# The first pair of blocks of the second part by eight out-products, with the weight sums formed beside them

## The chip, the cores and the metric

The kernel runs on one core of a Trainium2 chip. The metric is the device time of one execution in microseconds (us); lower is better. Engines are named as in the profile: PE is TensorE, DVE is VectorE, ACT is ScalarE, POOL is GpSimd, SP is SyncE, which issues most transfers.

## The reference

A Fourier layer is followed by two feed-forward layers over 6016 tokens of width 256. The change touches the last one only:

```python
def _moe2_ref(x, w_gate, w_val, w_out):
    g = x @ w_gate                          # 256 -> 1536
    silu = g * (1.0 / (1.0 + np.exp(-g)))
    val = x @ w_val                         # 256 -> 1536
    return (silu * val @ w_out).astype(np.float32)   # 1536 -> 256
```

## The kernel before

Every product is made in float32 precision by three matmuls over a split `x = hi + lo`, `w = hi + lo` (`mm3`: lo·hi, hi·hi, hi·lo; only the third reads the low half of x). The last layer, here called the second part, is computed with tokens in six pairs of blocks (`pairs`; a block has 512 tokens, in the last pair 448) and the 1536 inner rows in twelve slices of 128. One pair with one slice is a unit; `quads2` lists the 72 units, pair by pair, and unit q belongs to pair q // 12. Units 0 to 11 are the first pair, units 12 to 23 the second.

A unit makes gate and value of two blocks by seven products of Strassen's kind (`product(P, 1)` and so on), 21 matmuls, into three PSUM banks called P, T (`Tb`) and Q. In between ACT copies P to Q (the copy that starts Q, line 1297), T to `c7`, P to `cu`; DVE adds `h0 = T + cu` (line 1351) and `h1 = P + c7` (line 1368), ACT takes SiLU of both, and DVE multiplies them with Q and with P (`times2`). The last product, 3, of a unit and its `times2` are made in the next unit (`upper`). The two results of a unit are the gated values of its two blocks, and the second matrix w_out turns them into the output.

For w_out the kernel before uses, in all pairs but the last, seven products over two units at a time (an even one and the odd one behind it): three are made in the pair itself (`live`, 3 matmuls in an odd unit, 6 in an even one), and four are made in the pair behind it (`later`, 6 matmuls in each of its units, from tiles `mid` that `part2` splits). The sums of gated values come from DVE (`add_up`) and from accumulating transfers of POOL (`add_apart`, line 1251). Seven products need sums of the weights of w_out: `out_sums` (four DVE operations on 128x128 and one of ACT) and `out_parts` (two casts, two subtractions, two transfers) form them once, in the first pair. The last pair uses `plain` units: eight products, 12 matmuls in each unit (`share`), straight from the gated values: `parted` splits each into `hi` (ACT) and `lo` (DVE).

All order is written out by hand: each engine runs its instructions in the order of the code. `todo.send` sends one step of the split of the next pair's x per unit: first its load (`raw`, line 840), in the units behind it a cast `xo` or `xy` on ACT (line 806) in some and one subtraction on DVE in each. `fetch` loads a slice's weights into one of four slots.

Of the kernel before, what the change touches and what calls it, by code (L numbers as in the profile page):

```python
# [82 lines left out]
def fourier_moe_kernel(ctx: ExitStack, tc: tile.TileContext, x, lin, bias, w1, w2, fwd1, inv2, fwd2,  # L83
# [1149 lines left out]
    fourth = {}  # L1233

    def out_parts(k):
        g = G.pop(k)
        t = cv.tile([128, 4, 2, 128], F32R, tag="full", name="parts", bufs=2)
        f = fourth[k] = cv.tile([128, 2, 128], F32R, tag="s4", name="s4", bufs=1)
# [37 lines left out]

    def quad(q, before):
# [3 lines left out]
        old, i = p - 1, f  # L1281
        a = (p, k - 1) if k else (p - 1, NK - 1)
        if q == 0:
            fetch(F0 + 2)
            fetch(F0 + 3)
        P, T, Q = bank_p(F0 + q), one_bank(spot[0] + 3, [128, BLK], "Tb"), bank_q([128, BLK], "Q")
        product = multiply(B[len(pairs) + p], F0 + q, n)
        product(P, 1, start=True)
        if old >= 0:
            later(old, i, 0)  # L1290
        else:
            if q == 0:
                mark(Q)
                end = end_of()
                drain(2)
# [4 lines left out]
        if old >= 0:  # L1300
            later(old, i, 1)
        if odd:
            x1 = halve(p, k, "T1")
            (add_up if p else add_apart)(p, k, "T1", "T3")
            if a[0] >= 0:
                add_up(*a, "T2", "T1")
                add_apart(*a, "T4", "T2")
        elif a[0] >= 0:
            x2, x3 = halve(*a, "T4"), halve(*a, "T2")
            add_up(*a, "T3", "T2")  # L1310
        if old >= 0 and i % 3 == 2:
            phase(old, i // 3)
        if old >= 0:
            product(T, 7, start=True)
        c7 = ring2["c"]()[:, :n]
        nc.scalar.copy(c7, T[:, :n])
        if q == 0:
            end()
        product(Q, 2)
        if q == 0:  # L1320
            drain(2)
        product(P, 6)
        if p == 0:
            if odd and k < NK - 1:
                out_parts(k)
            if f in (0, 2, 4, 6, 8, 9):
                out_sums((f + 1) // 2)
            if f == NF - 1:
                ask(0, 0)
                ask(0, 1)  # L1330
        else:
            ask(old + (i + 2) // NF, (i + 2) % NF)
        if old + (i + 1) // NF >= 0:
# [3 lines left out]
        if q == 0:  # L1337
            drain(2)
        if odd:
            live(p, 1, k, slot[F0 + q - 1][:, 14:16], x1)  # L1340
            free.append(slot.pop(F0 + q - 1))
            fetch(F0 + q + 3)
            if f == NF - 1:
                then = begin(p)
        elif a[0] >= 0:
# [4 lines left out]
        h0 = take("h")  # L1350
        nc.vector.tensor_tensor(out=h0[:, :n], in0=T[:, :n], in1=cu, op=ALU.add)  # L1351
        nc.scalar.activation(h0[:, :n], h0[:, :n], AF.Silu)  # L1352
        if q == 0:
            drain(len(pending))
            lay_out_rest()
        if not odd and a[0] >= 0:
            live(a[0], 3, a[1], slot[F0 + q - 1][:, 16:18] if a[0] else fourth[a[1]], x3)
            free.append(slot.pop(F0 + q - 1))
            fetch(F0 + q + 3)
            if not k:  # L1360
                third(a[0])
            if f == NF - 2 and not p:
                out_parts(NK - 1)
        if q == 2:
            mark(one_bank(spot[0], [128, BLK], "D"))
        product(P, 5)
        h1 = take("h")
        nc.vector.tensor_tensor(out=h1[:, :n], in0=P[:, :n], in1=c7, op=ALU.add)  # L1368
        if q == len(quads2) - NF:
            d = home.pop()  # L1370
            spots["own"] = [d[:, 0], d[:, 1]]
            state["own"] = take("own")
        times2(state["own"][:, :n] if p == len(pairs) - 1 else U(p, ("T1", "T4")[odd], k), h0[:, :n], Q[:, :n], -1 if odd else 1)
        todo.send()
        nc.scalar.activation(h1[:, :n], h1[:, :n], AF.Silu)
# [3 lines left out]

    def plain(q, before):  # L1380

        p, f = quads2[q] if q < len(quads2) else (None, None)
        pb, old, i = len(pairs) - 1, len(pairs) - 2, f
        n = halves[pb]
        _, _, _, Pb, hb, last, _ = before
        w = slot[F0 + q - 1]

        def share(t, e, x):
            if q == len(quads2) - NF + 1:
                where = acc_bank  # L1390
                if t and e:
                    def where(shape, name):
                        return bank_p(F0 + q)
                acc[t, e] = where([128, BLK], f"acc{t}{e}")
            mm3(acc[t, e][:, :n], w[:, 14 + 2 * e], w[:, 15 + 2 * e], *x, q == len(quads2) - NF + 1, p is None)

        def parted(x):
            hi, lo = (take(c)[:, :n] for c in ("hi", "lo"))
            nc.scalar.copy(hi, x[:, :n])
            low(lo, x[:, :n], hi)  # L1400
            return hi, lo

        early = f == 1
# [3 lines left out]
        last(Pb, 3)  # L1407
        s1 = take("own")
        times2(s1[:, :n], hb[:, :n], Pb[:, :n], 1)
        if p is not None and not early:  # L1410
            later(old, i, 0)
            later(old, i, 1)
        x0 = parted(state["own"])
        if p is None:
            x1 = parted(s1)
            for t, x in enumerate((x0, x1)):
                for e in range(2):
                    share(t, e, x)
                    a = acc.pop((t, e))
                    if t and e:  # L1420
                        for o, c, copy, send in ((take("short"), slice(0, n // 2), nc.vector.tensor_copy, nc.sync),
                                                 (take("h"), slice(n // 2, n), nc.scalar.copy, nc.scalar)):
                            copy(o[:, c], a[:, c])
                            at = pairs[pb][0] + n
                            send.dma_start(out[e * 128 : e * 128 + 128, at + c.start : at + c.stop], o[:, c])
                    else:
                        o = spots[("one", "short", "short", "three")[2 * t + e]].pop()
                        (nc.vector.tensor_copy if e else nc.scalar.copy)(o[:, :n], a[:, :n])
                        send_out(pb, e, t, o)
            return None  # L1430
        k, odd = divmod(f, 2)
        if f == 1:
            add_up(old, NK - 1, "T2", "T1")
            add_apart(old, NK - 1, "T4", "T2")
        P, T, Q = Pb, one_bank(spot[0] + 3, [128, BLK], "Tb"), bank_q([128, BLK], "Q")
        P = one_bank(spot[0] + 1 + (F0 + len(quads2) - NF) % 2, [128, BLK], "P")
        product = multiply(B[len(pairs) + p], F0 + q, n)
        product(P, 1, start=True)
        nc.scalar.copy(Q[:, :n], P[:, :n])
        x1 = parted(s1)  # L1440
        if i % 3 == 2:
# [4 lines left out]
        share(0, 0, x0)  # L1446
        product(Q, 2)
        product(P, 6)
        if i + 1 < NF:
            part2(old, i + 1)  # L1450
        if i + 2 < NF:
# [3 lines left out]
        share(0, 1, x0)  # L1455
        product(T, 4)
        h0 = take("h")
        nc.vector.tensor_tensor(out=h0[:, :n], in0=T[:, :n], in1=cu, op=ALU.add)
        nc.scalar.activation(h0[:, :n], h0[:, :n], AF.Silu)
        product(P, 5)  # L1460
        h1 = take("h")
        nc.vector.tensor_tensor(out=h1[:, :n], in0=P[:, :n], in1=c7, op=ALU.add)
        share(1, 0, x1)
        share(1, 1, x1)
        free.append(slot.pop(F0 + q - 1))
        fetch(F0 + q + 3)
        state["own"] = take("own")
        times2(state["own"][:, :n], h0[:, :n], Q[:, :n], 1)
        nc.scalar.activation(h1[:, :n], h1[:, :n], AF.Silu)
# [6 lines left out]
    for q in range(len(quads2)):  # L1476
# [3 lines left out]
        before = (plain if q > len(quads2) - NF else quad)(q, before)  # L1480
# [62 lines left out]
```

## Time and profile before

| what | value |
| --- | --- |
| median of three runs (lowest, highest) | 1128.63 us (1128.04, 1129.52) |
| the profiled execution | 1129.65 us, its span 1127.9 us |
| PE, DVE, ACT busy, share of the span | 98%, 87%, 72% |
| units 1 to 11 | 622.69 to 696.09 us |
| units 12 to 23 | 696.09 to 779.80 us |

A unit's edge is where PE starts its first product in the timeline. A busy PE is not PE at its peak, since the recorded matmuls overlap: each stands for 0.38 us, while they start every 0.22 us where nothing waits. So gaps are read from the starts of matmuls in the timeline and not from busy time.

### The profile page before, as it was taken

What the parts mean: (1) busy time and instruction counts of PE and PEld (TensorE: products, weight loads), DVE (VectorE), ACT (ScalarE), POOL (GpSimd) and SP (SyncE); (2) the same over time, 40 slices, a digit from 0 to 9 for tenths busy, and PEclk for the clock granted to TensorE, in tenths of its full rate; (3) what the DMA queues carried; (4) which work ended last, traced back from release to release, by engine and by line L of the source; (5) the groups of instructions that cost most, each with busy time, mean ns of one, the idle gap of its engine ahead of it and who ended that gap; (6) DMA issues with size and microseconds to landing.
All of it is one profiled execution on the core that took longest, in us unless ns stands there. A gap on an engine that the chain in (4) does not pass through costs nothing.

```text
span 1127.9 us, 20014 instructions
## 1 busy us (share of the span) xinstructions
PE 1104.3 (98%) x7380; PEld 969.3 (86%) x7380; DVE 982.1 (87%) x1723; ACT 810.8 (72%) x1499; POOL 82.1 (7%) x117
## 2 busy tenths in 40 slices
PE   8999999999999999999999898999999999999998
PEld 8989888888888888888899776888888888888997
DVE  6878888999999999999988788899999999998665
ACT  4767676788787787877777666777777777677655
POOL 3000015200000000000000122000000000000000
PEclk9999999999999999999999999999999999999999
DMA  7757335864483573653654898877877877787561
GB/s 295 291 181 230 121 111 183 279 229 152 143 274 116 181 260 112 224 186 137 217 207 142 239 283 261 264 238 232 266 245 227 268 242 236 236 247 247 196 210 66
DMA packets 83929, 238.90 MB, mean 212 GB/s; under 512 B 8372, under 2 KB 30548, under 8 KB 72376
## 3 DMA queue, kind: packets, MB, share of 16 engines
q1 hardware_dynamic: 75472, 217.77, 57.3%
q0 software_dynamic: 8064, 19.66, 7.1%
q8 instruction: 58, 0.95, 0.3%
q14 instruction: 39, 0.32, 0.1%
q10 hardware_dynamic: 296, 0.20, 0.1%
HBM read 182.55 MB, written 45.61 MB: 202 GB/s over the span
## 4 chain that ended last, share of the span: by engine, by line
PE 79%; DVE 7%; issue 5%; DMA 5%; ACT 3%; POOL 1%; SPq 0%; POOLq 0%; ACTq 0%; DVEq 0%
PE acc L133 8%; PE acc L134 8%; PE acc L135 8%; PE P L947 7%; PE P L949 6%; PE P L948 6%; PE Tb L949 3%; PE Tb L947 3%; PE Tb L948 3%; DMA raw<-Xd 2%; PE p L462 2%; PE D L1174 2%; PE D L1173 2%; PE D L1172 2%; PE p L368 2%
## 5 line engine op out<-in xcount | busy, mean ns | idle before, releaser
L618 ACT CAST gated<-r 128x512 fp32r<-128x512 f32 (+1 forms) x160 | 98.1, 613 | 64.8 <-DVE r L995 63.3
L138 DVE TENSOR_TENSOR gated<-r,gated 128x512 fp32r<-128x512 f32 (+1 forms) x160 | 107.9, 674 | 24.1 <-ACT gated L618 19.6
L133 PE MATMUL acc<-gated,w_o 128*128 128x512 f32 (+1 forms) x320 | 120.4, 376 | 0.0
L135 PE MATMUL acc<-gated,w_o 128*128 128x512 f32 (+1 forms) x320 | 119.6, 374 | 0.0
L134 PE MATMUL acc<-gated,w_o 128*128 128x512 f32 (+1 forms) x320 | 119.6, 374 | 0.0
L1352 ACT ACTIVATE hv<-hv 128x512 f32<-128x512 f32 (+1 forms) x61 | 38.4, 630 | 98.2 <-DVE hv L1351 98.2
L991 ACT ACTIVATE r<-hold,consts 128x512 f32<-128x512 f32 (+1 forms) x120 | 85.5, 713 | 14.3 <-DVE hold L999 12.2
L947 PE MATMUL P<-xo,slot 128*128 128x512 f32 (+1 forms) x240 | 91.2, 380 | 2.8 <-DVE hold L999 1.2
L948 PE MATMUL P<-xo,slot 128*128 128x512 f32 (+1 forms) x240 | 88.8, 370 | 0.0
L949 PE MATMUL P<-xo,slot 128*128 128x512 f32 (+1 forms) x240 | 88.8, 370 | 0.0
L1251 POOL DMA_DIRECT2D units<-units x36 | 30.8, 893 | 785.5 <-PE P L949 419.5
L995 DVE SCALAR_TENSOR_TENSOR r<-r,hold 128x512 f32<-128x512 f32 (+1 forms) x120 | 80.8, 673 | 2.5 <-ACT r L991 1.4
L133 PEld LDWEIGHTS acc<-gated,w_o 128*128 128x128 f32 x320 | 60.5, 189 | 7.0
L135 PEld LDWEIGHTS acc<-gated,w_o 128*128 128x128 f32 x320 | 60.5, 189 | 6.8
L134 PEld LDWEIGHTS acc<-gated,w_o 128*128 128x128 f32 x320 | 60.5, 189 | 6.7
L1152 ACT CAST parts<-units 128x1024 fp32r<-128x1024 f32 x60 | 63.1, 1052 | 0.0
L1248 DVE TENSOR_TENSOR units<-units 128x512 f32<-128x512 f32 x84 | 55.7, 687 | 6.3 <-DMA units<-units 5.4
L947 PEld LDWEIGHTS P<-xo,slot 128*128 128x128 f32 x240 | 45.3, 189 | 14.6 <-DVE hv L1368 3.9
L1267 ACT CAST live<-units 128x512 fp32r<-128x512 f32 x90 | 53.5, 615 | 0.5 <-DVE units L1255 0.2
L949 PEld LDWEIGHTS P<-xo,slot 128*128 128x128 f32 x240 | 45.4, 189 | 4.3
L948 PEld LDWEIGHTS P<-xo,slot 128*128 128x128 f32 x240 | 45.4, 189 | 4.2
L1368 DVE TENSOR_TENSOR hv<-P,cc 128x512 f32<-128x512 f32 (+1 forms) x61 | 41.7, 683 | 4.5 <-PE P L949 4.5
(263 smaller groups left out, 3385.6 us busy)
## 6 DMA issues: line engine op xcount, KB each, us to landing
slot<-Wd SPq DMA_DIRECT2D x48, 1024.0 KB
slot<-Sd SPq DMA_DIRECT2D x40, 896.0 KB
slot<-Wd SPq DMA_DIRECT2D x24, 1152.0 KB
st<-in_w SPq DMA_DIRECT2D x68, 256.0 KB
chunk<-Vd SPq DMA_DIRECT2D x60, 256.0 KB
Wd<-slot SPq DMA_DIRECT2D x12, 1024.0 KB
units<-units POOLq DMA_DIRECT2D x36, 256.0 KB, 7.8
m<-in_fwd SPq DMA_DIRECT2D x12, 512.0 KB
```

Source lines behind the costliest of these rows:

```text
L133: nc.tensor.matmul(o, wl, xh, start=start, stop=False)
L134: nc.tensor.matmul(o, wh, xh, start=False, stop=False)
L135: nc.tensor.matmul(o, wh, xl, start=False, stop=stop)
L138: nc.vector.tensor_tensor(out=o, in0=full, in1=hi.bitcast(F32), op=ALU.subtract)
L618: nc.scalar.copy(hi[:, :n], g[:, :n])
L947: nc.tensor.matmul(o, wl, hi, start=start, stop=False, skip_group_check=not start)
L948: nc.tensor.matmul(o, wh, lo, start=False, stop=False, skip_group_check=not start)
L949: nc.tensor.matmul(o, wh, hi, start=False, stop=True, skip_group_check=not start)
L991: nc.scalar.activation(r[:, :n], x[:, :n], AF.Relu, bias=three)
L995: nc.vector.scalar_tensor_tensor(out=r[:, :n], in0=r[:, :n], scalar=6.0, in1=x[:, :n], op0=ALU.min, op1=ALU.mult)
L1152: nc.scalar.copy(hi, t[:, :, :n])
L1248: nc.vector.tensor_tensor(out=o, in0=o, in1=U(p, x, k), op=ALU.add)
```

## The change

Pair 0 now runs in `plain` units too. Its gated values go to `share` at once, 12 matmuls a unit, and nothing of pair 0 is left for pair 1: no `live`, `add_up`, `add_apart`, `part2` and `later` of pair 0, and none of the chunks of weight sums that pair 1 loaded for it. `out_sums` and `out_parts` stay in pair 0, one of them at the end of each unit. Unit 12 is a `quad` that also makes the last shares of pair 0 (`first`) and sends its four outputs. In pair 1, odd units take another bank for Q, and the SiLU of `h1` is put behind the next unit's copy to Q (`silu`, `seed`). One of two single matmuls that only mark a bank is dropped.

```diff
@@ fetch
+                whole = p in (0, len(pairs) - 1)
...
-            if stream[q][0] == 2 and p == len(pairs) - 1:
+            if stream[q][0] == 2 and whole:
                 nc.sync.dma_start(to[:, 16 * 128 :], src[:, 18 * 128 :])
@@ helpers
+    def outward(p, t, e):
+        n = halves[p]
+        o, a = (spots["one"][-1], spots["short"][-1], spots["short"][-2], spots["three"][-1])[2 * t + e], acc.pop((t, e))
+        (nc.vector.tensor_copy if e else nc.scalar.copy)(o[:, :n], a[:, :n])
+        send_out(p, e, t, o)
+
+    def silu(q, x):
+        def act():
+            nc.scalar.activation(x, x, AF.Silu)
+
+        if NF <= q + 1 < 2 * NF:
+            state["silu"] = act
+        else:
+            act()
+
+    def seed(q, P, Q, n):
+        nc.scalar.copy(Q[:, :n], P[:, :n])
+        state.pop("silu", lambda: None)()
@@ quad
-        P, T, Q = bank_p(F0 + q), one_bank(spot[0] + 3, [128, BLK], "Tb"), bank_q([128, BLK], "Q")
+        P, T = bank_p(F0 + q), one_bank(spot[0] + 3, [128, BLK], "Tb")
+        if p == 1 and odd and f < NF - 1:
+            Q = one_bank(spot[0], [128, BLK], "Q")
+        else:
+            Q = bank_q([128, BLK], "Q")
...
-        if old >= 0:
+        if waits:
             later(old, i, 0)
...
-        nc.scalar.copy(Q[:, :n], P[:, :n])
-        if before:
+        seed(q, P, Q, n)
+        if first:
+            x0 = parted(state["own"], n)
+            x1 = parted(upper_plain(before), n)
+        else:
             upper(before)
...
+        if first:
+            share(q, 0, 0, x0)
+            outward(0, 0, 0)
         product(Q, 2)
...
         h1 = second_sum(P, c7, n)
+        if first:
+            outward(0, 1, 1)
+            home.append(spots["double"])
@@ plain
+        if before:
+            s1 = upper_plain(before)
...
+        if before:
+            x0 = parted(spots["own"][0], n)
...
+        seed(q, P, Q, n)
+        if before:
+            x1 = parted(s1, n)
...
         product(T, 7, start=True)
...
+            share(q, 0, 0, x0)
         product(Q, 2)
         product(P, 6)
...
+            share(q, 0, 1, x0)
         product(T, 4)
         h0 = first_sum(T, cu, n)
...
         product(P, 5)
         h1 = second_sum(P, c7, n)
+        if q:
+            share(q, 1, 0, x1)
+            share(q, 1, 1, x1)
+            gone(q - 1)
+        times2(take("own")[:, :n], h0, Q[:, :n], 1)
+        state["own"] = spots["own"][-1]
+        todo.send()
+        silu(q, h1)
+        if not p:
+            (out_parts if odd else out_sums)(k)
@@ main loop
-        before = (plain if q > len(quads2) - NF else quad)(q, before)
+        before = (plain if q < NF or q in LAST else quad)(q, before)
```

On DVE, from the `h0` of unit 2 on, stood before (`outs<-` are the weight sums, `xo<-` is the step for the next pair, `units<-hv,P` the `times2` of product 3, `live`, `lows` and `hv<-units` the low halves):

```order
L1351 TENSOR_TENSOR hv<-Tb,cc 128x512
L1368 TENSOR_TENSOR hv<-P,cc 128x512
L1255 TENSOR_TENSOR units<-hv,Q 128x512
L138 TENSOR_TENSOR xo<-raw_7220,xo 128x512
L1257 SCALAR_TENSOR_TENSOR units<-hv,P 128x512
L138 TENSOR_TENSOR hv<-units,live 128x512
L1248 TENSOR_TENSOR units<-units 128x512
```

The same place on DVE now:

```order
L1321 TENSOR_TENSOR hv<-Tb,cc 128x512
L1327 TENSOR_TENSOR hv<-P,cc 128x512
L1254 TENSOR_TENSOR units<-hv,Q 128x512
L138 TENSOR_TENSOR xo<-raw_7217,xo 128x512
L1224 SCALAR_TENSOR_TENSOR outs<-hv 128x128
L1224 SCALAR_TENSOR_TENSOR outs<-outs,hv 128x128
L1222 TENSOR_TENSOR outs<-hv 128x128
L1222 TENSOR_TENSOR outs<-hv,outs 128x128
L1254 TENSOR_TENSOR units<-hv,P 128x512
L138 TENSOR_TENSOR live<-units,live 128x512
L138 TENSOR_TENSOR lows<-units,live 128x512
```

The weight sums, which stood ahead of `h0`, stand between the two `times2` now, and the low half of the first block's gated values (`live`) behind them.

On PE, from the last product of unit 2 (`P<-xy`, the product 5) to the first share of unit 3 stand now (`acc_7270` and `acc_7274` are the shares of the second block, `P<-gs` the product 3 of unit 2, then the products 1 and 7 of unit 3):

```order
L950 MATMUL P<-xy,slot 128x512
...
L135 MATMUL acc_7270<-hv,slot 128x512
...
L135 MATMUL acc_7274<-hv,slot 128x512
...
L950 MATMUL P<-gs,slot 128x512
...
L950 MATMUL P<-xy,slot 128x512
...
L950 MATMUL Tb<-xy,slot 128x512
L133 MATMUL acc_7246<-live,slot 128x512
L134 MATMUL acc_7246<-live,slot 128x512
L135 MATMUL acc_7246<-live,slot 128x512
```

Of each product's three matmuls only the last is shown. Fifteen matmuls, and two more of `acc_7246` itself, stand between the end of product 5 and the first reader of that low half; before, the units of pair 0 had no share there.

## Rows read from the trace of the kernel before

**Rows 1.** The page, part 1: busy time, share of the span, instructions.

```profile
PE 1104.3 (98%) x7380; PEld 969.3 (86%) x7380; DVE 982.1 (87%) x1723; ACT 810.8 (72%) x1499; POOL 82.1 (7%) x117
```

**Rows 2.** Windows: each engine's busy time, unit 1 to 11, then 12 to 23.

```profile
622.69:696.09 73.40, 64.46 (x282) 51.65 (x280) 61.37 (x114) 48.63 (x97) 17.63 (x23) 1.00 0.88 271
696.09:779.80 83.71, 82.54 (x379) 70.96 (x378) 76.57 (x111) 59.43 (x101) 4.87 (x6) 1.00 0.78 239
```

**Rows 3.** Timeline of PE: first and last of 185 matmuls without a wait.

```profile
741.17 0.38 PE L1173 MATMUL D<-parts,chunk 128*128 128x512 f32 x1
...
780.88 0.38 PE L1174 MATMUL D<-parts,chunk 128*128 128x512 f32 x1
```

**Rows 4.** Waits from 614 to 785 us: total, times, longest.

```profile
DVE units L1248 <- DMA units<-units: 5.4, 3, 2.4
...
PE Q L947 <- ACT Q L1297: 4.2, 10, 0.6
```

**Rows 5.** Timeline, all engines, around the end of unit 5.

```profile
654.08 0.38 PE L949 MATMUL Tb<-gs,slot 128*128 128x512 f32 x1
...
654.57 0.69 DVE L1351 TENSOR_TENSOR hv<-Tb,cc 128x512 f32<-128x512 f32 x1 [0.26 <-PE Tb L949]
...
655.18 0.68 DVE L1368 TENSOR_TENSOR hv<-P,cc 128x512 f32<-128x512 f32 x1
655.30 0.63 ACT L1352 ACTIVATE hv<-hv 128x512 f32<-128x512 f32 x1 [1.50 <-DVE hv L1351]
...
655.96 0.69 DVE L1257 SCALAR_TENSOR_TENSOR units<-hv,Q 128x512 f32<-128x512 f32 x1
...
657.17 0.68 DVE L1255 TENSOR_TENSOR units<-hv,P 128x512 f32<-128x512 f32 x1
```

**Rows 6.** Timeline of DVE: end of unit 0, weight sums, parts of them.

```profile
623.50 0.68 DVE L1255 TENSOR_TENSOR units<-hv,Q 128x512 f32<-128x512 f32 x1
...
647.75 0.28 DVE L1223 SCALAR_TENSOR_TENSOR outs<-hv 128x128 f32<-128x128 f32 x1
...
648.68 0.68 DVE L1351 TENSOR_TENSOR hv<-Tb,cc 128x512 f32<-128x512 f32 x1
...
690.55 0.28 DVE L138 TENSOR_TENSOR s<-outs,s 128x128 fp32r<-128x128 f32 x1
690.76 0.68 DVE L1368 TENSOR_TENSOR hv<-P,cc 128x512 f32<-128x512 f32 x1
```

**Rows 7.** Timeline: one engine handing on to the next.

```profile
643.20 0.63 ACT L1352 ACTIVATE hv<-hv 128x512 f32<-128x512 f32 x1 [1.50 <-DVE hv L1351]
...
643.74 0.60 ACT L806 CAST xo<-raw 128x512 fp32r<-128x512 f32 x1
...
644.25 0.63 ACT L1375 ACTIVATE hv<-hv 128x512 f32<-128x512 f32 x1
...
656.74 0.57 ACT L1297 COPY Q<-P 128x512 f32<-128x512 f32 x1 [0.21 <-DVE units L1257]
...
657.36 0.48 PE L947 MATMUL Q<-xy,slot 128*128 128x512 f32 x1 [0.31 <-ACT Q L1297]
...
691.50 0.48 PE L947 MATMUL P<-gs,slot 128*128 128x512 f32 x1 [1.94 <-DVE hv L1368]
```

**Rows 8.** Timeline of SP and ACT: the load of a pair's x.

```profile
623.37 0.57 SPq L840 DMA_DIRECT2D raw<-Xd  x1
...
629.12 0.60 ACT L806 CAST xo<-raw 128x512 fp32r<-128x512 f32 x1
...
704.17 0.34 SPq L1179 DMA_DIRECT2D out_t<-sums  x1
...
705.04 0.53 SPq L840 DMA_DIRECT2D raw<-Xd  x1
...
712.85 0.62 ACT L806 CAST xy<-raw 128x512 fp32r<-128x512 f32 x1 [0.96 <-DMA raw<-Xd]
```

**Rows 9.** Timeline of DVE: low part of a pair of units.

```profile
694.70 1.22 DVE L138 TENSOR_TENSOR parts<-units,parts 128x1024 fp32r<-128x1024 f32 x1
```

More of the change, by code (lines that the diff above doesn't have):

```diff
@@ L1275, in fourier_moe_kernel, with share, where, parted @@
     NK = KF2 // 2
+    NK = KF2 // 2
+    FIRST, LAST = range(NF + 1), range(len(quads2) - NF + 1, len(quads2) + 1)
+    def share(q, t, e, x):
+        n = halves[quads2[q - 1][0]]
+        if q % NF == 1:
+            where = acc_bank
+            if t and e:
+                def where(shape, name):
+                    return bank_p(F0 + q) if q in LAST else one_bank(spot[0], shape, name)
+            acc[t, e] = where([128, BLK], f"acc{t}{e}")
+        w = slot[F0 + q - 1]
+        mm3(acc[t, e][:, :n], w[:, 14 + 2 * e], w[:, 15 + 2 * e], *x, q % NF == 1, q % NF == 0)
+    def parted(x, n):
+        hi, lo = (take(c)[:, :n] for c in ("hi", "lo"))
+        nc.scalar.copy(hi, x[:, :n])
+        low(lo, x[:, :n], hi)
+        return hi, lo
+    def outward(p, t, e):
[3 more added lines that the diff above has]
+        send_out(p, e, t, o)
+    def gone(q):
+        free.append(slot.pop(F0 + q))
+        fetch(F0 + q + 4)
+    def silu(q, x):
[8 more added lines that the diff above has]
+        state.pop("silu", lambda: None)()
+    def first_sum(T, cu, n):
+        h = take("h")[:, :n]
+        nc.vector.tensor_tensor(out=h, in0=T[:, :n], in1=cu, op=ALU.add)
+        nc.scalar.activation(h, h, AF.Silu)
+        return h
+    def second_sum(P, c7, n):
+        h = take("h")[:, :n]
+        nc.vector.tensor_tensor(out=h, in0=P[:, :n], in1=c7, op=ALU.add)
+        return h
     def quad(q, before):
@@ L1303, in quad @@
             x1 = halve(p, k, "T1")
[L1304 to L1305 removed]
+            add_up(p, k, "T1", "T3")
+            if a[0] > 0:
                 add_up(*a, "T2", "T1")
                 add_apart(*a, "T4", "T2")
[L1308 removed]
+        elif a[0] > 0:
             x2, x3 = halve(*a, "T4"), halve(*a, "T2")
             add_up(*a, "T3", "T2")
[L1311 removed]
+        if waits and i % 3 == 2:
             phase(old, i // 3)
[L1313 removed]
+        if waits:
             product(T, 7, start=True)
@@ L1316, in quad @@
         nc.scalar.copy(c7, T[:, :n])
-        if q == 0:
-            end()
+        if first:
+            share(q, 0, 0, x0)
+            outward(0, 0, 0)
         product(Q, 2)
-        if q == 0:
-            drain(2)
         product(P, 6)
[L1323 to L1331, printed above, removed]
+        if waits:
             ask(old + (i + 2) // NF, (i + 2) % NF)
-        if old + (i + 1) // NF >= 0:
+        elif f == NF - 1:
+            ask(1, 0)
+            ask(1, 1)
+        if old + (i + 1) // NF > 0:
             part2(old + (i + 1) // NF, (i + 1) % NF)
@@ L1349, in quad @@
         product(T, 4)
[L1350 to L1359, printed above, removed]
+        h0 = first_sum(T, cu, n)
+        if first:
+            outward(0, 1, 0)
+            share(q, 1, 1, x1)
+            gone(q - 1)
+        elif not odd:
+            live(a[0], 3, a[1], slot[F0 + q - 1][:, 16:18], x3)
+            gone(q - 1)
             if not k:
                 third(a[0])
[L1362 to L1365, printed above, removed]
         product(P, 5)
-        h1 = take("h")
-        nc.vector.tensor_tensor(out=h1[:, :n], in0=P[:, :n], in1=c7, op=ALU.add)
+        h1 = second_sum(P, c7, n)
+        if first:
+            outward(0, 1, 1)
+            home.append(spots["double"])
         if q == len(quads2) - NF:
[L1370 to L1373, printed above, removed]
+            own()
+        times2(take("own")[:, :n] if p == len(pairs) - 1 else U(p, ("T1", "T4")[odd], k), h0, Q[:, :n],
+               -1 if odd and p < len(pairs) - 1 else 1)
+        state["own"] = spots["own"][-1]
         todo.send()
-        nc.scalar.activation(h1[:, :n], h1[:, :n], AF.Silu)
+        silu(q, h1)
         if f == NF - 1:
@@ L1378, in quad, with own, upper_plain @@
         return p, k, odd, P, h1, product, n
+    def own():
+        d = spots["double"] = home.pop()
+        spots["own"] = [d[:, 0], d[:, 1]]
+    def upper_plain(before):
+        _, _, _, P, h, product, n = before
+        product(P, 3)
+        s1 = take("own")
+        times2(s1[:, :n], h[:, :n], P[:, :n], 1)
+        return s1
     def plain(q, before):
         p, f = quads2[q] if q < len(quads2) else (None, None)
-        pb, old, i = len(pairs) - 1, len(pairs) - 2, f
+        pb = len(pairs) - 1 if q in LAST else 0
+        old, i = pb - 1 if p else -1, f
         n = halves[pb]
[L1385 to L1403, printed above, removed]
+        early = old > 0 and f == 1
         if early:
@@ L1406, in plain @@
             later(old, i, 1)
[L1407 to L1410, printed above, removed]
+        if before:
+            s1 = upper_plain(before)
+        if old > 0 and not early:
             later(old, i, 0)
             later(old, i, 1)
-        x0 = parted(state["own"])
+        if before:
+            x0 = parted(spots["own"][0], n)
         if p is None:
-            x1 = parted(s1)
+            x1 = parted(s1, n)
             for t, x in enumerate((x0, x1)):
                 for e in range(2):
-                    share(t, e, x)
-                    a = acc.pop((t, e))
+                    share(q, t, e, x)
                     if t and e:
+                        a = acc.pop((t, e))
                         for o, c, copy, send in ((take("short"), slice(0, n // 2), nc.vector.tensor_copy, nc.sync),
@@ L1445, in plain @@
         nc.scalar.copy(c7, T[:, :n])
-        share(0, 0, x0)
+        if q == 0:
+            end()
+            drain(2)
+        else:
+            share(q, 0, 0, x0)
         product(Q, 2)
         product(P, 6)
-        if i + 1 < NF:
+        if old > 0 and i + 1 < NF:
             part2(old, i + 1)
-        if i + 2 < NF:
+        if old > 0 and i + 2 < NF:
             ask(old, i + 2)
@@ L1454, in plain @@
         nc.scalar.copy(cu, P[:, :n])
-        share(0, 1, x0)
+        if q == 0:
+            drain(2)
+        else:
+            share(q, 0, 1, x0)
         product(T, 4)
-        h0 = take("h")
-        nc.vector.tensor_tensor(out=h0[:, :n], in0=T[:, :n], in1=cu, op=ALU.add)
-        nc.scalar.activation(h0[:, :n], h0[:, :n], AF.Silu)
-        product(P, 5)
[L1461 to L1469, printed above, removed]
+        h0 = first_sum(T, cu, n)
+        if q == 0:
+            drain(len(pending))
+            lay_out_rest()
+            own()
+        product(P, 5)
+        h1 = second_sum(P, c7, n)
+        if q:
+            share(q, 1, 0, x1)
+            share(q, 1, 1, x1)
+            gone(q - 1)
+        times2(take("own")[:, :n], h0, Q[:, :n], 1)
+        state["own"] = spots["own"][-1]
+        todo.send()
+        silu(q, h1)
+        if not p:
+            (out_parts if odd else out_sums)(k)
         return p, k, odd, P, h1, product, n
```

42 lines of the change are left out of this document (18 added, 24 removed).

## The prediction

> **What bounds the kernel now.** The page first: the reader is to see that PE is busy for 98% of the span [rows 1]. But that is an average, and busy matmuls overlap. So I took the timeline of PE and looked for a stretch without a wait: 185 matmuls start in 39.71 us, one every 0.2158 us [rows 3]. With this pitch any stretch can be divided into work and gaps. The windows give the two stages that the change touches, units 1 to 11 in 73.40 us and units 12 to 23 in 83.71 us, together 157.11 us [rows 2]. By the code the first holds 280 matmuls (six odd units of 24, five even ones of 27, one that marks a bank), the second 378 (twelve times 27, and 54 for `live`). 658 x 0.2158 = 142.0 us, so PE stands for 15.1 us here, 13.0 of it in units 1 to 11 (73.40 less 60.4). The waits say for what: for ACT's copy to Q in most units, and, behind DVE, for the accumulating transfer of POOL that DVE itself awaits [rows 4]. So pair 0 is held up by its chains, and pair 1 is close to bound by PE.
>
> **What the change does to PE's work.** Pair 0: eleven units of 33 matmuls (21 and 12 shares), 363. Unit 12 has 33 as well, the five even units behind it 27 each, the six odd ones 24: 312. Together 675, 17 more than before: 145.7 us, or +3.7 us. If the change fills the gaps it wins up to 11.4 us; so all hangs on the new gaps.
>
> **The join of two units in pair 0.** I walk along the end of a unit, with 0 where PE has issued the last matmul of product 5. Product 4 ended 0.65 earlier. DVE starts `h0` 0.49 after the start of product 4's last matmul, 0.27 after its end: at -0.38. `h1` follows 0.61 later, at 0.23; ACT begins the SiLU of `h0` 0.73 after `h0` began, and `times2` comes 0.66 behind that, at 1.01 [rows 5]. A DVE operation of 512 columns gives way to the next after 0.61 (657.17 less 655.96 is two of them) [rows 5], the four weight sums together take 0.93, the small subtraction of `out_parts` 0.21 [rows 6].
>
> Behind an even unit DVE then has: the step for the next pair (1.62), the weight sums (2.22), the `times2` of product 3 (3.15), the low half of the first block (3.76). PE starts 0.74 after the start of the DVE operation that it awaits (691.50, `h1` at 690.76) [rows 6, 7], so at 4.50. It gets there by itself after 17 matmuls, at 3.67. It stands for 0.83, and the first matmul after a wait is recorded with 0.48 us, not 0.38 [rows 3, 7]: 0.93 us. Each later unit waits anew, since `h0` hangs on product 4 behind the gap: five joins, 4.65 us.
>
> Behind an odd unit `out_parts` stands there. Its cast on ACT comes behind the SiLU of `h1`, and a SiLU gives way after 0.54, a cast `xo` after 0.51 [rows 7]. Without `xo` the cast starts at 1.49, DVE takes the parts at 2.22, the small one at 2.83, `times2` at 3.04, the low half at 3.65, PE at 4.39: 0.72 and 0.10, 0.82 us (two joins, behind units 5 and 7). With `xo` ahead of the SiLU (units 1, 3 and 9) the parts come at 2.60 and PE at 4.77: 1.2 us each. Behind unit 0 there are no shares yet to cover the join: `times2` at 623.50 [rows 6], the weight sums at 624.11, `times2` of product 3 at 625.04, the low half at 625.65, PE at 626.39; by itself it is there 11 matmuls after product 5 ended, which is the edge at 622.69 [rows 2], at 625.06: 1.33 and 0.10, 1.4 us. Sum for units 1 to 11: 1.4 + 4.7 + 3.6 + 1.6 = 11.3 us, hardly less than the 13.0 of before.
>
> **Units 12 to 23.** DVE loses twelve low parts of 1024 columns (1.22 us each) [rows 9], the sums of pair 0 and the wait for POOL's transfer, so its queue is no longer late; but PE loses 72 matmuls of `later`, which were the cover.
> - Unit 12: the SiLU put off stands ahead of the cast of the first block, so its low half comes at 3.86 and PE at 4.60 instead of 3.67: 1.0 us.
> - Unit 13: its copy to Q needs the bank from which DVE copies the last output of pair 0 (to 1.52); then the copy and 0.62 to PE [rows 7], 2.17 for 1.94: 0.3 us.
> - Unit 14: the load of x for pair 2 is issued on SP right behind that output, 0.43 later (two issues took 0.87 [rows 8]): at 1.98 after unit 12's product 5. In pair 1 of before it landed 7.81 later, and ACT stood for it [rows 8]; in pair 0, 5.75 us after issue the data were there [rows 8]. Now unit 13 is shorter by six matmuls. The `xo` cast holds the copy to Q behind it: landing + 0.51 + 0.62, or 8.9 to 10.9, for 7.45 on PE. Between 1.5 and 3.6 us; both rows have other loads beside them, I take the middle, 2.6. Its product 4 then waits another 0.5 for `c7`.
> - Units 16, 18, 20, 22: `c7` stands on ACT behind a cast that needs the `times2` of product 3, and comes 0.28 us late, 0.65 where an `xo` was ahead: 1.9 us in all. Odd units keep up.
> - Unit 24: in unit 23 DVE has two sums and a low part of 1024 before `h0`; with six matmuls of cover less `h1` is 0.75 us late.
>
> Sum: 1.0 + 0.3 + 3.1 + 1.9 + 0.75 = 7.0 us, where there were 2.1. If the cover holds better than I see, this is 2.5 (units 12 and 14 at their least).
>
> [...]
>
> **What costs nothing.** The second piece of a weight load, issued with the first for units 0 to 11, has two units until its use. POOL's accumulating transfers of pair 0 go, and nothing waits for POOL now. Fewer chunks are loaded in pair 1, which only helps SP. The four outputs of pair 0 go out in unit 12, ahead of a weight load on SP that is used two units later; only the load of x above is hurt. The rest of the kernel is the same.
>
> **Sum.** 145.7 of work, 11.3 and 7.0 of gaps: 164.0 us against 157.11, +6.9 us. The walk is made on the execution of 1129.65 us, which would be 1136.5; that lies 1.02 above the median of 1128.63, and I give the time against the median: **1135.5 us**.
>
> **Rivals.**
> - *The most loaded engine sets the stage* (faster). In pair 0 DVE has seven operations of 0.61 us and the weight sums, 5.2 us a unit, and PE 33 x 0.2158 = 7.1, so the gaps close, in pair 1 as well: -11.4 us, 1117.2 us. [...] For it: pair 0's DVE queue does get shorter than PE's. Against it: before, DVE was busy for 61.37 of 73.40 us and PE worked 60.4 of them [rows 2], so neither was full and PE still stood for 13 us; and seven instructions of DVE in a row lie between product 5 and the first share. It decides if the low half does not have to wait for the weight sums. Half of it (joins closed, pair 1 as walked: -4.4) gives 1124.2. Chance 0.04 and 0.10.
> - *The gaps stay as large as they were* (15.1 us): only the 17 matmuls count, +3.7, 1132.3 us. The pieces of my walk are separate, and some of them may be too long by a few tenths. Chance 0.12.
> - *No change*: the joins cost 0.15 less each (DVE's `times2` not held by ACT), the load lands early, and pair 1 keeps its cover but for units 12 and 14: 145.7 + 9.6 + 2.5 = 157.8, +0.7, 1129.3 us. Chance 0.14.
> - *The load of x is later still*, behind the weight load and four outputs: another 2 us, 1137.5. The output and the weight load ahead speak for it, the chunks that are no longer loaded against it. Chance 0.08.
>
> **How the numbers follow.** 0.2%, 2.3 us, is about what a measurement of this kernel can tell from no change. My forecast has 0.52, with the two rivals on its side 0.72; no change 0.14; faster 0.14. The likeliest case alone reaches from 1131 to 1138 us. Down to 1127.5 the range takes in the no-change case; it leaves out the faster rivals and a little above, about 0.2.
>
> **What would show it.** In the timeline of units 1 to 11 PE should stand for 0.8 to 1.2 us once a unit, ahead of the third matmul of the first share (`acc<-live`, line 135) and released by DVE's subtraction (line 138). Product 2 (Q) should no longer wait there. In units 12 to 23 there should be a single larger wait in unit 14, ACT's `xy` cast waiting for `raw<-Xd`, and small ones at product 4 of even units. I am wrong if the shares start without a wait: then DVE's chain is covered, or if the windows of units 1 to 11 come out near 79 us (without gaps) instead of 89.6.

## The result and the profile after

The changed kernel takes 1139.18 us (median of six runs, 1138.05 to 1139.79), the kernel before 1129.11 us beside it (six runs, 1128.04 to 1135.88): 1.0072 times as long, with an interval of 1.0043 to 1.0101. It is slower, as forecast. By the medians it is 10.1 us (0.9%). By the means it is 8.1 us (0.7%), which is what the ratio says, since two of the six runs of the kernel before took over 1135 us. The two profiled executions, 1129.65 and 1139.65 us, lie 10.0 apart. The forecast was 6.9 us more and 1135.5 us; 1139.18 lies above the 1138 us to which its likeliest case reached. The span of the profiled execution is 1137.9 us.

The page, part 1, of the changed kernel (as [rows 1]):

```profile
PE 1111.9 (98%) x7397; PEld 973.0 (86%) x7397; DVE 963.4 (85%) x1703; ACT 803.8 (71%) x1491; POOL 72.7 (6%) x105
```

There are 17 matmuls more, and DVE, ACT and POOL all do less. PE's share is 98% as before; the page alone would not tell that anything happened.

The windows of units 1 to 11 and 12 to 23 (as [rows 2]: stretch, length, busy time of PE, PEld, DVE, ACT and POOL, granted clock, DMA share, GB/s). The first edge is where PE's product 1 of unit 1 could have started, one pitch behind the last matmul of unit 0 at 622.12:

```profile
622.34:711.73 89.39, 82.06 (x364) 67.59 (x364) 59.31 (x113) 52.39 (x102) 6.29 (x10) 1.00 0.55 195
711.73:790.19 78.46, 73.46 (x314) 59.35 (x312) 61.03 (x96) 48.53 (x90) 4.79 (x7) 0.96 0.69 227
```

In the timeline 363 and 312 matmuls start in them, 78.3 and 67.3 us of work at the pitch of 0.2158 us. So the gaps are 11.1 and 11.1 us, and the two stages together take 167.85 us for 157.11 before, 10.7 more. The sum had put 89.6 and 74.4 us. In the second line the granted clock is 0.96: not all of what is missing there is a wait.

The timeline of the changed kernel around the end of unit 2 (start, duration, engine, line, operation; in brackets the idle time and who ended it):

```profile
638.85 0.69 DVE L1254 TENSOR_TENSOR units<-hv,Q 128x512 f32<-128x512 f32 x1
639.45 0.68 DVE L138 TENSOR_TENSOR xo<-raw,xo 128x512 fp32r<-128x512 f32 x1
...
640.05 0.28 DVE L1224 SCALAR_TENSOR_TENSOR outs<-hv 128x128 f32<-128x128 f32 x1
...
640.37 0.29 DVE L1224 SCALAR_TENSOR_TENSOR outs<-outs,hv 128x128 f32<-128x128 f32 x1
640.58 0.28 DVE L1222 TENSOR_TENSOR outs<-hv 128x128 f32<-128x128 f32 x1
...
640.78 0.28 DVE L1222 TENSOR_TENSOR outs<-hv,outs 128x128 f32<-128x128 f32 x1
...
640.99 0.68 DVE L1254 TENSOR_TENSOR units<-hv,P 128x512 f32<-128x512 f32 x1
...
641.29 0.38 PE L134 MATMUL acc<-live,slot 128*128 128x512 f32 x1
...
641.58 0.68 DVE L138 TENSOR_TENSOR live<-units,live 128x512 fp32r<-128x512 f32 x1
...
642.32 0.48 PE L135 MATMUL acc<-live,slot 128*128 128x512 f32 x1 [0.66 <-DVE live L138]
```

DVE works through its queue without a pause: the step for the next pair, four weight sums, the `times2` of product 3, the low half. PE has done the two matmuls that read the high half and stands 0.81 us longer than a pitch for the low one. This is the wait that the walk foresaw, with the same cause and at the same place. It comes ten times, behind each of units 1 to 10, with 0.69 to 0.87 us.

The waits of the changed kernel from 614 to 795 us (as [rows 4]: engine, line and tile, total, times, longest):

```profile
PE Q L948 <- ACT Q L1316: 4.2, 1, 4.2
ACT xy L806 <- DMA raw<-Xd: 4.2, 1, 4.2
...
PE acc L135 <- DVE lows L138: 2.5, 4, 0.7
...
PE acc L135 <- DVE hv L138: 2.1, 3, 0.7
...
PE acc L135 <- DVE live L138: 1.8, 3, 0.7
```

The view counts only time in which no matmul is on record. In it the copy to Q held PE ten times before; now it does so once, in unit 14, and for 4.2 us. The three rows of L135 are the ten joins. SP, ACT and PE in the timeline there:

```profile
721.16 0.33 SPq L868 DMA_DIRECT2D slot<-Wd  x1
...
722.04 0.53 SPq L840 DMA_DIRECT2D raw<-Xd  x1
...
724.41 0.33 SPq L868 DMA_DIRECT2D slot<-Wd  x1
...
730.65 0.62 ACT L806 CAST xy<-raw 128x512 fp32r<-128x512 f32 x1 [4.16 <-DMA raw<-Xd]
...
731.18 0.58 ACT L1316 COPY Q<-P 128x512 f32<-128x512 f32 x1
...
731.81 0.80 PE L948 MATMUL Q<-xo,slot 128*128 128x512 f32 x1 [4.19 <-ACT Q L1316]
732.40 0.63 PE L949 MATMUL Q<-xo,slot 128*128 128x512 f32 x1
732.82 0.63 PE L950 MATMUL Q<-xo,slot 128*128 128x512 f32 x1
```

The load of x is issued between two weight loads and is there 8.6 us later; ACT stands for it, and the copy to Q stands behind the cast. PE then waits 4.35 us. What follows is the second thing to see: the next matmuls are recorded with 0.63 us, not 0.38, and start 0.43 apart. The windows around it, with the granted clock in the third column from the right:

```profile
722.00:726.00 4.00, 3.97 (x18) 3.29 (x19) 2.84 (x5) 2.24 (x5) 0.00 (x0) 1.00 1.01 309
726.00:730.00 4.00, 1.62 (x8) 1.08 (x6) 1.12 (x2) 0.49 (x1) 0.00 (x0) 1.00 1.02 416
730.00:732.00 2.00, 0.19 (x1) 0.19 (x2) 0.69 (x1) 1.35 (x3) 0.00 (x0) 0.52 0.83 350
732.00:734.00 2.00, 2.00 (x5) 1.64 (x6) 1.57 (x3) 1.76 (x4) 0.00 (x0) 0.50 0.02 8
734.00:736.00 2.00, 2.00 (x6) 1.55 (x6) 1.01 (x2) 0.76 (x2) 0.00 (x0) 0.50 0.00 0
736.00:738.00 2.00, 2.00 (x9) 1.69 (x8) 0.69 (x1) 0.00 (x1) 0.00 (x0) 0.77 0.00 0
```

The last matmul ahead of the wait ended at 727.6; from 730 on the granted clock is 0.52 and then 0.50, 0.77 in the last window and 1.00 in the two microseconds behind it. From 726.5 to 737.9, 21 matmuls start where 53 would fit: 6.9 us are lost, 4.35 in the wait and 2.5 in slow matmuls. The DMA engines are full (1.01, 1.02) from 722 to 730. The DMA view of 720 to 732 says with what:

```profile
DMA packets 844, 3.80 MB, mean 317 GB/s; under 512 B 77, under 2 KB 77, under 8 KB 589
...
slot<-Wd SPq DMA_DIRECT2D x1, 1152.0 KB
raw<-Xd SPq DMA_DIRECT2D x1, 1024.0 KB
slot<-Wd SPq DMA_DIRECT2D x1, 1024.0 KB
out_t<-hv SPq DMA_DIRECT2D x1, 256.0 KB
out_t<-sums SPq DMA_DIRECT2D x1, 256.0 KB
```

The load of x shares the engines with a weight load and an output ahead of it and a weight load behind it. The 3.80 MB at the 416 GB/s of the full window are 9.1 us (an estimate), about as long as from 721.16 to the landing at 730.65.

### The profile page after: what moved, and what is told of

It reads as the page before. It is cut to its first block, busy times and chain, and to the rows that moved or that the text cites. A ratio compares the mean times of both kernels' runs of the same rounds, so it can differ in the third digit from the quotient of the medians.

```text
span 1137.9 us, 19968 instructions
## 1 busy us (share of the span) xinstructions
PE 1111.9 (98%) x7397; PEld 973.0 (86%) x7397; DVE 963.4 (85%) x1703; ACT 803.8 (71%) x1491; POOL 72.7 (6%) x105
## 4 chain that ended last, share of the span: by engine, by line
PE 78%; DVE 12%; ACT 4%; DMA 3%; issue 2%; POOL 0%; DVEq 0%; ACTq 0%; SPq 0%; POOLq 0%
PE acc L135 8%; PE acc L133 8%; PE acc L134 8%; PE P L948 7%; PE P L950 6%; PE P L949 6%; PE Tb L948 3%; PE Tb L950 3%; PE Tb L949 3%; DMA raw<-Xd 2%; PE p L462 2%; PE p L368 2%; PE Q L948 2%; PE Q L949 2%; PE Q L950 2%
## 5 line engine op out<-in xcount | busy, mean ns | idle before, releaser
L1322 ACT ACTIVATE hv<-hv 128x512 f32<-128x512 f32 (+1 forms) x72 | 44.8, 622 | 107.0 <-DVE hv L1321 107.0
L135 PE MATMUL acc<-gated,w_o 128*128 128x512 f32 (+1 forms) x320 | 119.6, 374 | 0.0
L1321 DVE TENSOR_TENSOR hv<-Tb,cc 128x512 f32<-128x512 f32 (+1 forms) x72 | 48.6, 675 | 33.9 <-PE Tb L950 33.9
L135 PEld LDWEIGHTS acc<-gated,w_o 128*128 128x128 f32 x320 | 60.5, 189 | 6.9
L133 PE MATMUL acc<-live,slot 128*128 128x512 f32 (+1 forms) x156 | 58.9, 378 | 0.8 <-ACT live L1292 0.8
L134 PE MATMUL acc<-live,slot 128*128 128x512 f32 (+1 forms) x156 | 58.4, 374 | 0.0
L948 PEld LDWEIGHTS P<-xo,slot 128*128 128x128 f32 x240 | 45.4, 189 | 13.5 <-DVE hold L1000 3.0
L1316 ACT COPY Q<-P 128x512 f32<-128x512 f32 (+1 forms) x72 | 40.8, 566 | 20.3 <-PE P L950 16.7
L1327 DVE TENSOR_TENSOR hv<-P,cc 128x512 f32<-128x512 f32 (+1 forms) x72 | 48.4, 672 | 6.1 <-PE P L950 6.1
L1153 ACT CAST parts<-units 128x1024 fp32r<-128x1024 f32 x48 | 50.5, 1052 | 0.0
L950 PEld LDWEIGHTS P<-xo,slot 128*128 128x128 f32 x240 | 45.5, 190 | 4.4
```

Source lines behind the costliest of these rows:

```text
L133: nc.tensor.matmul(o, wl, xh, start=start, stop=False)
L134: nc.tensor.matmul(o, wh, xh, start=False, stop=False)
L135: nc.tensor.matmul(o, wh, xl, start=False, stop=stop)
L948: nc.tensor.matmul(o, wl, hi, start=start, stop=False, skip_group_check=not start)
L950: nc.tensor.matmul(o, wh, hi, start=False, stop=True, skip_group_check=not start)
L1153: nc.scalar.copy(hi, t[:, :, :n])
```

## The experiments

Two theories stood after that. The first: the loss sits in the two places above, DVE's order at the joins (some 9 us) and the load of x with the slow clock behind it (some 7 us), and either can be taken away alone. The rival: the stage is bound by something behind them (17 matmuls more, PSUM banks, the SiLU put off), so that a gap that is closed opens again elsewhere. On the chips of the experiments the kernel before had medians of 1131.73 and 1130.99 us and single runs from 1128.75 to 1136.19, so ratios to it on the same chip are compared.

**The load early.** Only the step that issues the load of x for pair 2 moves, from the end of unit 12 to its start:

```diff
 quad
+        if first:
+            todo.send()
...
-        todo.send()
+        if not first:
+            todo.send()
```

> Edit: the load of x for the third pair is issued at the start of unit 12, ahead of the four outputs and a weight load on SP, instead of behind them. Theory (the chain raw, xy cast, copy to Q): the wait of 4.35 us in unit 14 goes, and with it the stretch at the lower granted clock (12 matmuls at 0.43 us, 2.5 us): 6 to 7 us less than the changed kernel, about 1132.5 us, clock 1.0 in the window of unit 14. Rival (the transfer is slow because the queues are full, wherever it is issued): the landing stays 8 us or more behind the need, at most 2 us less, above 1137 us.

Measured: 1133.92 us, 1.0013 [1.0000, 1.0026]. The load is issued at 712.23, 4.4 us ahead of the first output of pair 0. The load and its first reader in the timeline of this kernel, and two of its windows:

```profile
712.23 0.53 SPq L840 DMA_DIRECT2D raw<-Xd  x1
...
725.83 0.60 ACT L806 CAST xy<-raw 128x512 fp32r<-128x512 f32 x1
```

```profile
724.00:728.00 4.00, 4.00 (x20) 3.25 (x19) 3.08 (x6) 2.69 (x5) 0.00 (x0) 1.00 0.99 377
728.00:732.00 4.00, 3.95 (x18) 3.02 (x17) 3.15 (x6) 2.46 (x5) 0.00 (x0) 1.00 0.40 140
```

ACT's cast has no wait, PE has none in unit 14 but 0.32 us at product 4 (the late `c7`), and the granted clock stays at 1.00. The joins are what they were, 0.69 to 0.88 us. Against the changed kernel (1.0072 and, on the other chip, 1.0077) this is 0.6%, some 7 us: the wait of 4.35 alone would give 0.4%. The intervals of the ratios are too wide to tell the two apart by time alone. The traces do: from product 1 of unit 12 to product 1 of unit 24 this kernel takes 72.17 us (711.16 to 783.33) for 78.46, 6.3 less, so the slow stretch went with the wait. What the trace does not show is when the load landed, since nothing waited for it.

**The weight sums covered.** Only `out_sums` and `out_parts` move, from the end of a unit of pair 0 to the place ahead of its copy to `cu`, where DVE waits for PE anyway:

```diff
 plain
+        if not p:
+            (out_parts if odd else out_sums)(k)
         cu = ring2["c"]()[:, :n]
         nc.scalar.copy(cu, P[:, :n])
...
         silu(q, h1)
-        if not p:
-            (out_parts if odd else out_sums)(k)
```

> Edit: in pair 0 the weight sums and their halves stand ahead of ACT's copy to cu, so behind the low halves of a unit and ahead of its h0, where DVE stood for 2.5 us; not at the unit's end. Theory (the order on DVE between product 5 and the first share costs the joins): the waits at the third matmul of the first share (0.7 to 0.9 us in each of units 2 to 12) go, since the low half then starts 2.84 after product 5 and PE needs it at 3.67: 9 to 11 us less, about 1129 us. Rival (DVE or ACT are loaded too much in pair 0, wherever the sums stand): the waits move to h0 or to product 3 and at least half of the 10 us stays, above 1134 us.

Measured: 1130.86 us, 0.9990 [0.9979, 1.0001]. Timeline of DVE and PE in this kernel, from the weight sums of unit 4 to the first share of unit 5:

```profile
647.87 0.28 DVE L1222 TENSOR_TENSOR outs<-hv,outs 128x128 f32<-128x128 f32 x1
...
649.35 0.69 DVE L1321 TENSOR_TENSOR hv<-Tb,cc 128x512 f32<-128x512 f32 x1 [1.20 <-PE Tb L950]
...
651.95 0.68 DVE L1254 TENSOR_TENSOR units<-hv,P 128x512 f32<-128x512 f32 x1
...
652.55 0.69 DVE L138 TENSOR_TENSOR lows<-units,live 128x512 fp32r<-128x512 f32 x1
...
653.18 0.38 PE L134 MATMUL acc<-live,slot 128*128 128x512 f32 x1
```

DVE idles for 1.20 us between the last sum and product 4, so the sums cost nothing, and the low half starts 0.63 us ahead of PE's second matmul of the share, not behind it. All ten waits of the joins are gone; one of 0.24 us is left in units 2 to 11. They were 8.1 us beyond the pitch, and 0.10 more each for the late second matmul: 9.1. The time falls by 0.8% against the changed kernel, 9.3 us. Unit 14 is untouched: 4.48 us of wait, and behind it seven starts of matmuls 0.43 us apart.

**Both.** The two edits together.

> Both edits together: sums covered and load early. Theory (two separate causes): both gains add, 16 to 17 us less than the changed kernel, about 1122.5 us, which is 6 us below the kernel before. Rival (one hides the other, or PE's gaps reappear at other places): less than 13 us of gain, above 1126 us.

Measured: 1124.09 us, 0.9938 [0.9926, 0.9950]. The gains add up (0.6 and 0.8 to 1.4%). From unit 1 to unit 23 waits beyond 0.2 us are left in few places, the largest 0.94 in unit 1 and 0.58 in unit 12. In the traces these units take 151.9 us for 167.85, 15.9 less. Behind them a little did open: from product 1 of unit 24 to the end this kernel takes 349.8 us for 347.7, and most of that is PE's waits for the copy to Q behind the next loads of x, 0.88, 1.18 and 0.62 us beyond the pitch for 0.37, 0.54 and none. The largest of them:

```profile
877.39 0.48 PE L948 MATMUL Q<-xo,slot 128*128 128x512 f32 x1 [1.02 <-ACT Q L1316]
```

The gain, some 15 us, is above the 13 us that the rival theory allowed, and the kernel is faster than the one before: the rival theory falls, but for these 2 us.

**Matmuls into the wait.** Twelve more matmuls into an idle bank, in unit 14 ahead of product 2, so that PE does not stand as long while the load is as late as before:

```diff
+        if q == NF + 2:
+            idle = one_bank(spot[0], [128, BLK], "idle")
+            for _ in range(12):
+                nc.tensor.matmul(idle, slot[F0 + q][:, 0], B[len(pairs) + 1][1][:, 0], start=True, stop=True)
         product(Q, 2)
```

> Edit: the changed kernel with 12 extra matmuls (2.6 us of PE work into a bank that is not read) in unit 14, ahead of product 2, in the gap of 4.35 us. Theory (the long idle lowers the granted clock): the wait for the copy to Q still ends at the same time, but PE stands for only 1.8 us, the clock stays at 1.0 and the 12 matmuls behind the gap start every 0.216 us: 2.4 us less, about 1136.8 us. Rival (those matmuls are slow for another reason, such as transfers that land then): they stay at 0.43 us and the time stays at 1139.2 us.

Measured: 1139.32 us, 1.0063 [1.0050, 1.0076]. Timeline of PE in unit 14, and windows as above:

```profile
731.84 0.48 PE L948 MATMUL Q<-xo,slot 128*128 128x512 f32 x1 [2.00 <-ACT Q L1316]
```

```profile
730.00:732.00 2.00, 0.16 (x1) 0.17 (x2) 0.69 (x1) 1.32 (x3) 0.00 (x0) 1.00 0.61 256
732.00:734.00 2.00, 2.00 (x9) 1.45 (x9) 1.55 (x3) 1.75 (x4) 0.00 (x0) 1.00 0.02 8
```

The load lands as late, and product 2 starts as late. But PE stands for 2.0 us where it stood for 4.2, the clock stays at 1.00, and the matmuls behind follow at the pitch. From there to the first product of unit 24 it takes 56.36 us for 58.38, 2.0 less. So the slow matmuls go with the granted clock (0.50), and in this case with PE having stood so long: they follow the wait in all three traces that have one over 4 us (4.2, 4.3 and 4.65), and neither here, with 2.0, nor in any trace without such a wait does the clock fall in these units. In the time of the whole kernel it doesn't show, and the rival's figure of 1139.2 us came out: the load was later (product 2 starts 4.92 us beyond the pitch after the last regular matmul, for 4.35), and in unit 24 a chunk of weights came 1.38 us too late:

```profile
790.23 0.45 PE L1173 MATMUL D<-parts,chunk 128*128 128x512 f32 x1 [1.22 <-DMA chunk<-Vd]
```

This is one trace; in two of the four executions the mean granted clock is 0.998, and where it fell in them is not on record.

**The changed kernel again**, unaltered, on the chip of the experiments that follow.

> The changed kernel unaltered, beside the others on one chip: 0.7% above the kernel before, with the waits of 0.7 to 0.9 us at the first share in units 2 to 12 and one wait over 4 us in unit 14 behind which matmuls start every 0.43 us.

Measured: 1139.83 us, 1.0077 [1.0061, 1.0092]. The joins are 0.69 to 0.88 us again, and unit 14 stands for 4.81:

```profile
731.86 0.48 PE L948 MATMUL Q<-xo,slot 128*128 128x512 f32 x1 [4.65 <-ACT Q L1316]
```

The slow stretch follows, but a shorter one: PE goes on at the pitch, and two matmuls later come eight starts 0.43 us apart, 1.7 us lost for 2.5. The two places are no chance of one execution; the size of the slow stretch varies.

**The SiLU at once**, on top of both edits: `silu` no longer puts it behind the next copy to Q.

```diff
 silu
-        if NF <= q + 1 < 2 * NF:
-            state["silu"] = act
-        else:
-            act()
+        act()
```

> Both edits of before (sums covered, load early), and the SiLU of h1 no longer put behind the next unit's copy to Q. Theory (the deferral helps the copy to Q of units 13 to 23 and hurts unit 12): unit 12's wait of 0.8 us goes; in pair 1 the copy to Q starts 0.5 us later in units behind an xy cast, which still is in time for product 2 (0.4 us of room), so within 1 us of the kernel with both edits. Rival (the deferral is what keeps pair 1 going, as before, where PE waited for this copy in 10 units): waits of 0.3 to 0.6 us ahead of product 2 in most units 13 to 23, 3 to 5 us more.

Measured: 1124.65 us, 0.9942 [0.9929, 0.9955], the same as with both edits. The wait in unit 12 goes (0.58 us), and so do the waits at product 4; but product 2 waits again, by 0.62 in units 14, 16 and 22 and by 0.15 to 0.26 in the others of 13 to 23. Putting the SiLU off moves the waits of pair 1 from one product to the other and gives nothing that can be measured.

**One bank for Q**, on top of both edits: odd units of pair 1 use the bank of Q as the even ones do.

```diff
 quad
-        if p == 1 and odd and f < NF - 1:
-            Q = one_bank(spot[0], [128, BLK], "Q")
-        else:
-            Q = bank_q([128, BLK], "Q")
+        Q = bank_q([128, BLK], "Q")
```

> Both edits of before, and odd units of pair 1 use the same bank for Q as the even ones. Theory (the copy to Q then waits for the multiplication that reads the old Q, which ends 1.7 us after product 5, and PE wants product 2 at 1.94, the copy taking 0.6): waits of 0.4 us ahead of product 2 in each of units 13 to 23, about 4.5 us more than with both edits. Rival (the bank does not matter, DVE is early enough): no new wait, within 1 us.

Measured: 1129.19 us, 0.9979 [0.9967, 0.9990], 0.4% or some 4.6 us more than both edits alone (by their ratio on the other chip). Waits for the copy to Q stand in every unit of 13 to 23, 0.85 and then 0.46 and 0.25 by turns, 4.4 us in sum for 0.5 with two banks; one of them in the timeline of this kernel:

```profile
718.07 0.48 PE L948 MATMUL Q<-xo,slot 128*128 128x512 f32 x1 [0.31 <-ACT Q L1316]
```

So the second bank is a part of the change that pays, and the prediction had not given it a term of its own.

**What the traces point to.** Both edits; unit 12 does not get a SiLU put off from unit 11; unit 1 makes product 3 of unit 0 behind its own products 1 and 7; even units of pair 1 copy `c7` ahead of the casts; and each pair's load of x goes out at the start of the pair's first unit.

```diff
-        if NF <= q + 1 < 2 * NF:
+        if NF < q + 1 < 2 * NF:
...
+        if not f:
+            todo.send()
...
+        soon = not waits and not odd and not first
+        if soon:
+            c7 = ring2["c"]()[:, :n]
+            nc.scalar.copy(c7, T[:, :n])
...
+        late = q == 1
+        if before and not late:
             s1 = upper_plain(before)
...
+        if late:
+            product(T, 7, start=True)
+            s1 = upper_plain(before)
```

> Both edits, and four small ones for the gaps that are left: unit 11's SiLU not put off (0.8 us at unit 12), product 3 of unit 0 behind products 1 and 7 of unit 1 (0.9 us), the copy to c7 ahead of the casts in even units of pair 1 (5 waits of 0.3 us), and the load of x at the start of the first unit of every pair (0.5 to 0.9 us each in pairs 2 to 4). Theory (each gap goes where its own cause is taken away): 4 to 5 us less than both edits, 1.0% below the kernel before. Rival (PE's gaps move elsewhere): less than 2 us.

Measured: 1120.99 us (1118.39 to 1125.12), 0.9912 [0.9895, 0.9928]: 0.9% faster than the kernel before and 1.6% faster than the change as it was made. The largest wait left between unit 1 and unit 24 is 0.51 us, in unit 24. The profiled execution is the slowest of the six, 1125.12 us. It lost time ahead of these units, where PE stood 1.84 us for a load, and the clock fell while it ran the 86 small matmuls behind:

```profile
105.39 1.97 PE L578 MATMUL p<-inv_sb,ct 48*64 48x47 f32 x86 [1.84 <-DMA ct<-Cd]
```

```profile
106.00:107.00 1.00, 1.00 (x58) 1.00 (x51) 0.53 (x1) 0.44 (x2) 0.00 (x0) 0.59 1.03 416
107.00:108.00 1.00, 1.00 (x15) 0.83 (x10) 0.17 (x2) 0.62 (x2) 0.00 (x0) 0.50 1.04 420
```

## Why the prediction was right, and where not

- **PE's work, 145.7 us**: right. 675 matmuls start between the edges, at the pitch of [rows 3].
- **Joins in pair 0, 11.3 us**: right, 11.1 by the windows. Behind even units 0.93 was put, and 0.81 and 0.10 came; behind units 5 and 7 0.82 for 0.69 and 0.10; behind units with `xo` ahead of the SiLU 1.2 for 0.87, 0.10 and 0.17 more ahead of the share's first two matmuls. At the end of unit 0 the place was wrong: the 1.4 us was put at the first share, but PE stood for `h1` ahead of product 3, 0.94, and then 0.24 at the share, with 0.10 behind each. That this comes to 1.4 as well is luck. The weight sums experiment shows the cause: with the sums and their parts elsewhere the waits are gone.
- **Product 2 no longer waits in pair 0**: right; the waits of [rows 4] for ACT's copy to Q are no longer there.
- **Unit 14, 2.6 us and 0.5 for `c7`**: the step that failed, in two ways. The load landed 8.6 us after its issue, where the prediction took the middle between 5.75 and 7.81 [rows 8]; with 8.6 its own formula gives 4.3, and 4.35 came. The rival of a later load (1137.5) had the place and the direction. And the 2.5 us of matmuls at a granted clock of 0.50 had no term at all: nothing in [rows 2] showed a clock under 1.00, and the walk asked only how long PE would stand, not what PE would be when it came back. The 0.5 for `c7` did not appear, since unit 14 was late already; with the load early 0.32 of it did. Unit 14 cost 6.9 us, not 3.1: 3.8 of the 3.9 us by which the gaps of the sum were too small.
- **The rest of units 12 to 23 and unit 24, 3.9 us**: 4.2 came between the edges. Unit 12 has 0.58 and 0.19, unit 13 0.25, product 4 of units 16 to 22 0.20 to 0.32, unit 23 0.26 and 0.13, with 0.10 more for each. The wait for `h1` of unit 23, put at 0.75, was 0.51 and stands ahead of product 3, behind the edge.
- **The sum**: +10.7 us in these stages for +6.9, of which the whole profiled execution shows 10.0. The 0.7 that the rest gave back lies half ahead of unit 1 (622.34 for 622.69) and half from product 1 of unit 24 on (347.7 us for 348.1).

The middle that the prediction took for the load of x had little behind it. The trace of before holds three more loads of this kind for which ACT stood. They landed 7.74, 7.49 and (the last pair's, which is shorter) 7.38 us after their issue, and with any of them the term would have been over 3 us. The first of them:

```profile
788.00 0.53 SPq L840 DMA_DIRECT2D raw<-Xd  x1
...
795.74 0.62 ACT L806 CAST xo<-raw 128x512 fp32r<-128x512 f32 x1 [0.92 <-DMA raw<-Xd]
```

Of the rivals, *the most loaded engine sets the stage* did not come, but what it named was there to be had. In pair 0 the engine with the most busy time is PE (82.06 of 89.39 us), and yet it stood for 11 us, since DVE, busy for 59.31, did its short work in the wrong order. Only the order made the difference: the same instructions, otherwise placed, came to 0.9% under the kernel before. That this is near what the rival had put (1117.2 us for 1128.63 is 1.0%) is in part luck. In the traces the last kernel takes 150.8 us (626.41 to 777.24) from unit 1 to unit 24, 6.3 less than the kernel before where the rival had 11.4 less, and 2.0 less behind them, in pairs that the rival had left alone.

The load of x in unit 14, 8.6 us from its issue to its landing, shared the engines with 2.7 MB of other transfers. The sharing fits the windows (a DMA share of 1.01 and 1.02 from 722 to 730) and the DMA view, but no run took the other transfers away, so it is not shown that they alone made it late.

Left open: where before's 13 us of gaps in pair 0 would have gone under other small edits, and why single executions of one kernel differ by up to 8 us. Two things on record bear on the second. The time that PE takes to reach unit 1 differs from trace to trace, from 620.8 to 626.4 us. And the trace of before, with a mean granted clock of 1.000, is not the usual one: in 34 of its 40 executions beside the experiments the mean is 0.995 to 0.999, so a stretch under 1.00 is in them too, and no trace shows where. With both edits it is 1.000 in five of six executions. A part of what the experiments gained on the kernel before may be this.

## What to carry to other kernels

When work moves into a stage, walk each engine's queue between one product's end and the first reader behind it: operations that fit easily into the engine's idle time still cost most of their length when they stand in a chain that PE awaits (0.93 us of sums, 0.82 us of wait), and nothing where the engine waits for PE (with the sums covered, DVE still idled for 1.20 us behind them). Issue a load by the time at which its first reader stands on the path, with the slowest landing that the trace shows, not the middle, and ahead of outputs and weight loads that nobody awaits soon. Price a long wait of PE as the wait and what PE does slowly after it, here 4.35 and 2.5 us.

## What the runs showed of the hardware

- In one wait of PE of 4.2 us (the changed kernel, unit 14) the granted clock went from 1.00 to 0.50, and it stayed there for some five us of work: ten starts of matmuls 0.43 us apart, 2.5 us lost. Behind waits of 4.32 us (the weight sums covered) and 4.65 us (the changed kernel again) it fell only after PE had gone on, for seven and eight such starts, 1.7 us lost each. In these stages waits of 2.0 us (the matmuls into the wait) and less left it at 1.00, those of the joins (0.69 to 0.88 us) too. That is no safe length: in the last kernel's trace it fell to 0.59 and then 0.50 behind a wait of 1.84 us, among the 86 small matmuls that followed.
- A load of one megabyte, issued between two weight loads of about the same size, took 8.6 us to land, with the DMA engines full (a share of 1.01 and 1.02), at 309 and 416 GB/s in the two windows. In the three other traces with the load at this place (the weight sums covered, the matmuls into the wait, the changed kernel again) it took 8.7 to 9.2 us. The loads of x for other pairs for which ACT stood took 7.4 to 7.8 us in the trace of before, 7.0 to 7.7 in that of the changed kernel and 8.0 and 8.1 with one bank for Q.
